# One fused attention and MoE kernel: whole-bank score units, maxima ahead of exponentials, a planner that takes turns at PSUM banks, ten native items

## Chip, cores and metric

The kernel runs on one core of one Trainium2 chip. The metric is device time in microseconds (us): the median over the runs of one kernel. TensorE is called PE here, VectorE DVE, ScalarE ACT, GpSimd POOL and SyncE SP, as in the profile.

## What is computed

Causal-by-block attention for 4 batches of 8 heads (576 positions, head size 64, blocks of 64), then two feed-forward layers over the 2304 tokens: one that takes the largest of three products, one with h * cos(h).

```python
scores = scale * np.matmul(q, k.transpose(0, 1, 3, 2))
mask = (pos[:, None] // 64) >= (pos[None, :] // 64)
scores = np.where(mask, scores, -1e9)
attn = np.exp(scores - scores.max(-1, keepdims=True))
attn = attn / (attn.sum(-1, keepdims=True) + 1e-09)
x = attn @ v                                   # to (2304, 512)
h = np.maximum(np.maximum(x @ w1, x @ w2), x @ w3)   # 512 to 768
x = h @ w_out                                  # 768 to 512
h = x @ w_in                                   # 512 to 2048
out = (h * np.cos(h)) @ w_out2                 # 2048 to 512
```

All inputs are float32, the weights pass as pairs of 32-bit words.

## The kernel before

**Items.** Attention is cut into 32 items: 4 batches, two halves of the query blocks, 4 pairs of heads. `load` fetches q, k and v of an item, two items ahead. `prep` makes operands for the scores. An item with a number under `NATIVE` (line 555) is native: q and k stay float32, k is scaled in place, and a score product is one float32 matmul, which the trace shows as two instructions. Any other item is split: q and k are each divided into a high and a low part in fp32r (`qh`, `ql`, `kh`, `kl`), and a score product is three matmuls, high x high, high x low, low x high. Native q and k (`qnat`, `knat`, two buffers each) lie in the pool `cv_start`. Items 8 to 11, the second batch's first half, have four blocks and 64 to 256 score columns each, 640 in all. Native or not, weights of the MoE layers are also taken apart into high and low parts (`convert`: tiles `raw`, `t`, `whi`, `wlo`), on DVE and ACT, beside attention.

**Scores.** `scores` goes through the tiles of an item. A tile is one or two banks of PSUM (slots `SA`, two banks, and `SB`, one bank), and holds the scores of one to three query blocks. For each block, PE's matmuls are recorded first (in one unit for each block and bank: instructions that the planner keeps together). Then, block by block, DVE takes the maximum (`top`) and ACT the exponential with its row sum (`prob`). Then the rows are scaled by their sums, transposed on PE (`tb`, copied to `pt`), multiplied with v (`X`) and written to `xhi`, `xlo` or, by way of `xs`, to memory.

**Filler.** The first MoE layer's matmuls for 512 tokens (`psm`, two banks) can start once attention has given those tokens; the first 512 are complete after item 7. From then on they fill PE between the parts of attention. Their evictions go to `hm`, in pool `wk`. `wk` is opened when `cv_start` is closed, and a pool closes only after all users of its tiles.

**The planner.** Nothing runs in the order in which it is recorded. `Plan` records operations with their reads and writes, gives each a cost (`price`), and lists them forward and backward in eight passes (`forward`, `backward`); the shortest plan is emitted, each engine's instructions in the planned order. Before the change, two operations depend on each other when the ranges of a tile that they touch overlap and one of them writes. Two reads never do, and a matmul into other columns of a bank doesn't depend on a read of that bank. The semaphores of the program itself are put in by the framework behind the planner, after the emitted order. `COLD` is the time before which the planner counts PE as slow.

Of the kernel before, what the change touches and what calls it, by code (L numbers as in the profile page):

```python
# [19 lines left out]
P = 128  # L20
# [109 lines left out]
class Plan:  # L130
    CROSS = 150.0
    EARLY = 130000.0
    SWITCH = 350.0
    COLD = 7600.0
    SLOW, CROWD, LANDING = 9000.0, 50000.0, 1000.0
    WEIGHT = {"DVE": 2.5, "ACT": 1.0, "POOL": 100.0}

# [38 lines left out]
    def record(self, engine, real, method, args, kw):  # L176
        if self.unit_op == "new" or self.unit_op is None:
            o = self.op(engine)
            if self.unit_op == "new":
                self.unit_op = o  # L180
        else:
            o = self.unit_op
        out = [kw["out"] if "out" in kw else args[0]] + ([kw["accum_out"]] if "accum_out" in kw else [])
        given = [v for v in list(args) + list(kw.values()) if isinstance(v, View)]
        outs = [v for v in out if isinstance(v, View)]
        ins = [v for v in given if not any(v is w for w in outs)]
        for v, write in [(v, False) for v in ins] + [(v, True) for v in outs]:
            b = v.buf
            o.deps |= {x for x, lo, hi in (b.writes + b.reads if write else b.writes)
                       if x is not o and lo <= v.hi and v.lo <= hi}  # L190
            if write:
                if v.hi - v.lo == v.n - 1 and v.rows == b.shape[0] and self.unit_op is None:
                    b.reads = [x for x in b.reads if x[1] < v.lo or x[2] > v.hi]
                    b.writes = [x for x in b.writes if x[1] < v.lo or x[2] > v.hi]
                b.writes.append((o, v.lo, v.hi))
            else:
                b.reads.append((o, v.lo, v.hi))
            if not b.ops or b.ops[-1] is not o:
                b.ops.append(o)
        cost, late, port = self.price(engine, method, outs, ins, kw)  # L200
        o.cost += cost
        o.port = o.port or port
        o.late = max(o.late, late)
        o.bufs |= {v.buf for v in given}
        o.calls.append(self.caller(real, method, args, kw))
        return o
# [39 lines left out]
    def price(self, engine, method, outs, ins, kw):  # L246


        if engine == "SP":
            tiles = outs + ins  # L250
            return 600.0, 2000.0 + sum(v.n * v.rows * 4 for v in tiles[:1]) / 340.0, False
        n = outs[0].n
        if engine == "PE":
            late = 190.0
            if method == "transpose":
                return 109.0, late, False
            dt = ins[0].buf.dt
            if dt == F32:
                return (4 * n / 2.4 + 13) / (2 if outs[0].rows == 64 else 1), late, False
            load = ins[0].n / 1.2  # L260
            return (max(n / 2.4 + 3, 65.0) if dt == BF16 else max(n / 2.4 + 13.5, load)), late, False
        psum = any(v.buf.psum for v in outs + ins)
        if method == "tensor_reduce":
            n = ins[0].n
        spread = 120.0 * (outs[0].hi - outs[0].lo + 1 > n)
        ptr = isinstance(kw.get('scale'), View) or len([v for v in ins if v.n == 1]) > 0
        if engine == "ACT":
            scaled = isinstance(kw.get("scale"), View)
            return (n * 0.833 + spread + (55 if psum else 100) + 95 * ("bias" in kw) + 95 * scaled
                    + 93 * ("accum_out" in kw)), 112.0, False  # L270
        if engine == "DVE":
            sb = [v for v in ins if not v.buf.psum]
            fast = method in ("tensor_copy", "tensor_scalar", "memset") and not psum
            two = method in ("tensor_tensor", "scalar_tensor_tensor") and len(sb) > 1
            if method == "reciprocal":
                return 70.0 + 5 * n, 100.0, False
            if method == 'memset':
                return n * 0.82, 88.0, True
            return n * (0.52 if fast else 1.04) + 68 + spread + (65.0 if fast and len([v for v in ins if v.n == 1]) else 0), 88.0, fast or two
        return (n * 3.3 + 75 if method == "tensor_tensor" else max(400.0, n * 1.04 + 195)), 45.0, method != "memset"  # L280


    ENGINES = ("PE", "DVE", "ACT", "POOL", "SP")
# [17 lines left out]
    def forward(self, rank):  # L301
# [6 lines left out]
        end, chosen, bus, port = {}, {}, 0.0, 0.0  # L308

        def finish(o, start, stop):  # L310
            end[o] = (start, stop)
            for u in self.users[o]:
                missing[u] -= 1
                if not missing[u]:
                    release(u)

        def release(o):
# [14 lines left out]
            load[o.engine] += o.cost  # L332
            heapq.heappush(waiting[o.engine], (at, rank[o], o.order, o))

        for o in self.ops:
            if not o.deps:
                release(o)
        while len(end) < len(self.ops):
            best = None
            for e in free:  # L340
                while waiting[e] and waiting[e][0][0] <= free[e]:
                    at, r, order, o = heapq.heappop(waiting[e])
                    heapq.heappush(ready[e], (r, order, at, o))
                if ready[e]:
                    t, pick = free[e], ready[e][0]
                    if pick[3].port and port > t:
                        others = [x for x in ready[e] if not x[3].port]
                        if others:
                            pick = min(others)
                        else:  # L350
                            t = port
                elif waiting[e]:
                    pick = waiting[e][0]
                    t = max(pick[0], port if pick[3].port else 0.0)
                else:
                    continue
                if best is None or t < best[0]:
                    best = (t, e, pick)
            assert best, "the plan has a cycle"
            t, e, pick = best  # L360
            o = pick[3]
            if ready[e]:
                ready[e].remove(pick)
                heapq.heapify(ready[e])
            else:
                heapq.heappop(waiting[e])
            free[e] = t + self.spent(o, t)
            load[e] -= o.cost
            stop = free[e] + o.late
            if o.port:  # L370
                port = free[e]
            if e == "SP":
                bus = max(bus, t + o.cost)
                bus += (o.late - 2000.0) * (1.22 if bus < self.SLOW else 1.0)
                stop = bus + 2000.0
            finish(o, t, stop)
# [76 lines left out]
def fused_kernel(tc, qk, v2, w1, w2, w3, wout, w_in2, w_out2, out):  # L453
    B, HP, _, S = qk.shape
# [10 lines left out]
    R = Plan(tc)  # L465
# [16 lines left out]
    NROT = 3  # L482
    top = [[const.tile([P, 1], F32, f"top{i}_{j}") for j in range(5)] for i in range(NROT)]
# [6 lines left out]
    parts = [(0, 512)]  # L490
# [51 lines left out]
    for first, last, *tiles in (  # L542
# [5 lines left out]
        f = Half()  # L548
# [3 lines left out]
        f.nj = (last + 1) // 2  # L552
        f.order = [(j, b) for j in range(f.nj) for b in f.blocks if 64 * (b + 1) > 128 * j]
        HALF.append(f)
    NATIVE = 8

    items = []
    for b in range(B):
        for half in range(2):
            for pair in range(HP):  # L560
                it = Item()
# [41 lines left out]
    def scores(it):  # L603
# [4 lines left out]
        for banks, parts in f.tiles:  # L608
            if banks == 2:
                s = ps_x.tile([P, 2, 512], F32, "SA", tag="SA", bufs=1)  # L610
            else:
                s = ps_x.tile([P, 1, 512], F32, "SB" if parts[0][0] % 2 == 0 or it.half else "SA", tag="SB" if banks == 1 else "SA", bufs=1)
            started = {}
            for b, c0, n, c in parts:
                i = b - f.first
                qs = slice(i * P, i * P + P)
                for bank in range(c):
                    ks = slice(bank * n, bank * n + n)
                    prods = [(it.q[:, qs], it.k[:, ks])] if it.native else [
                        (it.qh[:, qs], it.kh[:, ks]), (it.qh[:, qs], it.kl[:, ks]), (it.ql[:, qs], it.kh[:, ks])]  # L620
                    with R.unit():
                        for x, (q, k) in enumerate(prods):
                            R.tensor.matmul(s[:, bank, c0:c0 + n], q, k, start=bank not in started and x == 0,
                                            stop=x == len(prods) - 1, skip_group_check=True)
                        if started.setdefault(bank, R.unit_op) is not R.unit_op:
                            R.unit_op.deps.add(started[bank])
            for b, c0, n, c in parts:
                i = b - f.first
                part = s[:, :, c0:c0 + n] if c == 2 else s[:, 0, c0:c0 + n]
                bias = top[it.n % NROT][i]  # L630
                R.vector.tensor_reduce(bias, part, axis=AX.XY if c == 2 else AX.X, op=ALU.max, negate=True)
                p = prob[b][:, 0:n * c]
                if c == 2:
                    p = p.rearrange("p (c n) -> p c n", c=2)
# [279 lines left out]
    banks = {}  # L914
# [90 lines left out]
```

## Time and profile before

| | us |
|---|---|
| median of 3 runs | 893.03 (892.97 to 894.29) |
| the profiled execution | 893.89 |
| its span, first to last instruction | 892.1 |
| PE busy | 874.9 (98%) |
| DVE busy | 551.4 (62%) |
| ACT busy | 436.3 (49%) |

A busy share is a mean over the whole span: attention and the first MoE layer fill the first 390 us or so, the second MoE layer the rest. PE's busy time counts matmuls from start to modelled end, so an idle gap in it is real, and a busy stretch can still hold lost turns. The waits name who released an engine; a wait of PEld is that of a weight load, which stands in PE's queue in front of its matmul.

### The profile page before, as it was taken

The numbers are of one execution on the slowest core, as the hardware profiler recorded it, in microseconds if no ns is written. First come the engines' busy times: TensorE is split into PE (matmuls) and PEld (weight loads), VectorE is DVE, ScalarE is ACT, GpSimd is POOL, SyncE is SP. The second block draws the span as 40 slices with busy tenths as digits, with TensorE's granted clock in tenths as the row PEclk, the third lists the DMA queues.
The fourth block names the chain that finished last, engine by engine and source line by source line (L and its number), as shares of the span: only waits on it lengthen the run. The fifth ranks groups of instructions, "written<-read, shape, count | busy, mean of one in ns | idle before, by whom it ended". The sixth has DMA issues, their size and how long they took to land.

```text
span 892.1 us, 12461 instructions
## 1 busy us (share of the span) xinstructions
PE 874.9 (98%) x4626; PEld 722.9 (81%) x4626; DVE 551.4 (62%) x1092; ACT 436.3 (49%) x955; POOL 1.2 (0%) x12
## 2 busy tenths in 40 slices
PE   7899999999999999999999999999999999999998
PEld 5567877888878787878889888888888888888897
DVE  5999988874566725629332697655465455455454
ACT  6987687863677717756221543332233223322333
POOL 0000000000000000000000000000000000000000
PEclk9999999999999999999999999999999999999999
DMA  7655645661245702545040751110001000100000
GB/s 238 207 170 171 194 133 189 225 225 71 84 136 189 246 25 59 152 158 173 27 142 6 291 198 50 48 48 1 0 25 48 1 0 1 48 1 0 24 25 24
DMA packets 42396, 90.33 MB, mean 101 GB/s; under 512 B 5728, under 2 KB 15456, under 8 KB 42336
## 3 DMA queue, kind: packets, MB, share of 16 engines
q1 hardware_dynamic: 42336, 89.54, 30.3%
q8 instruction: 36, 0.59, 0.3%
q14 instruction: 24, 0.20, 0.1%
HBM read 69.07 MB, written 20.45 MB: 100 GB/s over the span
## 4 chain that ended last, share of the span: by engine, by line
PE 88%; DVE 6%; ACT 3%; issue 1%; DMA 1%; POOLq 0%; SPq 0%; POOL 0%; ACTq 0%; DVEq 0%
PE psm L211 53%; PE po L211 22%; PE X L211 4%; PE SA L211 4%; PE tb L211 3%; PE SB L211 3%; DVE top L211 2%; ACT prob L211 2%; DVE t L211 2%; DMA q<-qk 1%; DVE prob L211 0%; ACT pt L211 0%; DVE wlo L211 0%; DVE whi L211 0%; DVE ql L211 0%
## 5 line engine op out<-in xcount | busy, mean ns | idle before, releaser
L211 PE MATMUL psm<-yh,w_in 128*128 128x512 f32 (+1 forms) x640 | 194.0, 368 | 0.0
L211 PE MATMUL po<-w_out,gh 128*128 128x512 f32 x576 | 177.8, 390 | 0.0
L211 ACT ACTIVATE th<-th,halfpi 128x512 f32<-128x512 f32 (+1 forms) x80 | 54.6, 683 | 188.8 <-DVE th L211 188.8
L211 PE MATMUL psm<-xhi,whi 128*128 128x512 f32 (+1 forms) x360 | 135.3, 376 | 1.2 <-ACT hm L211 0.7
L211 PEld LDWEIGHTS psm<-yh,w_in 128*128 128x128 f32 x640 | 117.1, 188 | 20.5
L211 PE MATMUL psm<-xlo,whi 128*128 128x512 f32 (+1 forms) x360 | 132.7, 369 | 0.0
L211 PE MATMUL psm<-xhi,wlo 128*128 128x512 f32 (+1 forms) x360 | 132.7, 369 | 0.0
L211 PEld LDWEIGHTS po<-w_out,gh 128*128 128x128 f32 x576 | 107.1, 188 | 21.4
L211 PE MATMUL psm<-yl,w_in 128*128 128x512 f32 (+1 forms) x320 | 117.7, 368 | 0.0
L211 PE MATMUL po<-w_out,gl 128*128 128x512 f32 x288 | 112.0, 389 | 0.0
L211 DVE TENSOR_SCALAR th<-psm 128x512 int32<-128x512 f32 (+1 forms) x80 | 51.0, 638 | 76.1 <-PE psm L211 75.9
L211 DVE TENSOR_TENSOR th<-psm,th 128x512 f32<-128x512 f32 (+1 forms) x80 | 51.0, 638 | 53.8 <-ACT th L211 53.8
L211 DVE TENSOR_TENSOR hm<-psm,hm 128x512 f32<-128x512 f32 (+1 forms) x60 | 38.2, 636 | 68.4 <-PE psm L211 67.9
L211 PEld LDWEIGHTS psm<-xhi,whi 128*128 128x128 f32 x360 | 68.0, 189 | 11.8 <-ACT hm L211 1.2
L211 PEld LDWEIGHTS psm<-xhi,wlo 128*128 128x128 f32 x360 | 67.9, 189 | 11.6
L211 PEld LDWEIGHTS psm<-xlo,whi 128*128 128x128 f32 x360 | 68.0, 189 | 9.8 <-DVE xlo L211 0.2
L211 DVE TENSOR_TENSOR gl<-th,gh 128x512 fp32r<-128x512 f32 (+1 forms) x80 | 50.9, 636 | 38.4 <-ACT gh L211 38.4
L211 ACT CAST gh<-th 128x512 fp32r<-128x512 f32 (+1 forms) x76 | 44.1, 580 | 55.7 <-DVE th L211 55.7
L211 PEld LDWEIGHTS psm<-yl,w_in 128*128 128x128 f32 x320 | 60.3, 189 | 10.6
L211 PEld LDWEIGHTS po<-w_out,gl 128*128 128x128 f32 x288 | 54.1, 188 | 11.3
L211 PE MATMUL tb<-ident,prob 128*128 128x128 f32 x400 | 59.7, 278 | 1.2 <-ACT pt L211 0.6
L211 ACT COPY pt<-tb 128x512 f32<-128x512 f32 (+1 forms) x94 | 51.9, 568 | 16.4 <-PE tb L211 15.9
(96 smaller groups left out, 1322.4 us busy)
## 6 DMA issues: line engine op xcount, KB each, us to landing
raw<-w SPq DMA_DIRECT2D x18, 512.0 KB, 3.5
raw<-w_in SPq DMA_DIRECT2D x16, 512.0 KB, 3.7
raw<-w_out SPq DMA_DIRECT2D x16, 512.0 KB, 4.3
vr<-v SPq DMA_DIRECT2D x16, 320.0 KB, 3.5
kept_in<-both SPq DMA_DIRECT2D x10, 512.0 KB, 3.7
w_in<-kept_in SPq DMA_DIRECT2D x10, 512.0 KB, 9.1
out<-osb SPq DMA_DIRECT2D x18, 256.0 KB, 2.0
y<-hm SPq DMA_DIRECT2D x16, 256.0 KB, 2.5
```

What stands on the lines that cost most here:

```text
L211: return lambda: getattr(real, method)(*[value(a) for a in args], **{k: value(a) for k, a in kw.items()})
```

## The change

Five edits. (1) In `scores` all matmuls of a bank become one unit, whatever blocks they belong to; only the first of them carries the start flag. (2) The maxima of all blocks of a tile are recorded ahead of all exponentials. (3) In `record`, an access to a PSUM tile counts as one to the whole tile, and a read depends on earlier reads by other engines, so the plan lets engines take turns at it. (4) `NATIVE` goes from 8 to 10: items 8 and 9 are native too. (5) Figures of the planner: `COLD` 7600 to 7400, another price for POOL's memset and affine_select; and a counter in place of a length, with no effect on the plan.

```diff
-    COLD = 7600.0
+    COLD = 7400.0
...
             b = v.buf
-            o.deps |= {x for x, lo, hi in (b.writes + b.reads if write else b.writes)
-                       if x is not o and lo <= v.hi and v.lo <= hi}
+            lo, hi = (0, len(b.index)) if b.psum else (v.lo, v.hi)
+            o.deps |= {x for x, x0, x1 in (b.writes + b.reads if write else b.writes)
+                       if x is not o and lo <= x1 and x0 <= hi}
+            if b.psum:
+                o.deps |= {x for x, _, _ in b.reads if x.engine != engine}
...
-        return (n * 3.3 + 75 if method == "tensor_tensor" else max(400.0, n * 1.04 + 195)), 45.0, method != "memset"
+        if method in ("memset", "affine_select"):
+            return n * 1.2 + 90.0, 45.0, False
+        return (n * 3.3 + 75 if method == "tensor_tensor" else max(400.0, n * 1.04 + 195)), 45.0, True
...
-    NATIVE = 8
+    NATIVE = 10
...
-            started = {}
-            for b, c0, n, c in parts:
-                i = b - f.first
-                qs = slice(i * P, i * P + P)
-                for bank in range(c):
-                    ks = slice(bank * n, bank * n + n)
-                    prods = [(it.q[:, qs], it.k[:, ks])] if it.native else [
-                        (it.qh[:, qs], it.kh[:, ks]), (it.qh[:, qs], it.kl[:, ks]), (it.ql[:, qs], it.kh[:, ks])]
-                    with R.unit():
+            for bank in range(s.dims[0][1] if banks == 2 else 1):
+                with R.unit():
+                    first = True
+                    for b, c0, n, c in parts:
+                        ks = slice(bank * n, bank * n + n)
+                        i = b - f.first
+                        qs = slice(i * P, i * P + P)
+                        prods = [(it.q[:, qs], it.k[:, ks])] if it.native else [
+                            (it.qh[:, qs], it.kh[:, ks]), (it.qh[:, qs], it.kl[:, ks]), (it.ql[:, qs], it.kh[:, ks])]
                         for x, (q, k) in enumerate(prods):
-                            R.tensor.matmul(s[:, bank, c0:c0 + n], q, k, start=bank not in started and x == 0,
-                                            stop=x == len(prods) - 1, skip_group_check=True)
-                        if started.setdefault(bank, R.unit_op) is not R.unit_op:
-                            R.unit_op.deps.add(started[bank])
+                            R.tensor.matmul(s[:, bank, c0:c0 + n], q, k, start=first, stop=x == len(prods) - 1,
+                                            skip_group_check=True)
+                            first = False
             for b, c0, n, c in parts:
                 i = b - f.first
                 part = s[:, :, c0:c0 + n] if c == 2 else s[:, 0, c0:c0 + n]
                 bias = top[it.n % NROT][i]
                 R.vector.tensor_reduce(bias, part, axis=AX.XY if c == 2 else AX.X, op=ALU.max, negate=True)
+            for b, c0, n, c in parts:
+                i = b - f.first
+                part = s[:, :, c0:c0 + n] if c == 2 else s[:, 0, c0:c0 + n]
+                bias = top[it.n % NROT][i]
                 p = prob[b][:, 0:n * c]
```

## Rows read from the trace of the kernel before

**Rows 1.** The page, busy time: engine, us, share of the span, instructions.
```profile
PE 874.9 (98%) x4626; PEld 722.9 (81%) x4626; DVE 551.4 (62%) x1092; ACT 436.3 (49%) x955; POOL 1.2 (0%) x12
```

**Rows 2.** Three windows: length, busy time and instructions of each engine, PE clock, DMA.
```profile
0.00:75.00 75.00, 64.62 (x384) 46.73 (x384) 63.80 (x170) 62.86 (x169) 1.17 (x12) 0.98 0.62 205
75.00:400.00 325.00, 321.79 (x1864) 262.36 (x1865) 216.10 (x462) 211.64 (x515) 0.00 (x0) 1.00 0.46 149
400.00:892.00 492.00, 488.46 (x2380) 413.82 (x2378) 271.50 (x462) 161.83 (x274) 0.00 (x0) 1.00 0.16 54
```

**Rows 3.** Chain of waits, first 80 us: shares by engine and tile.
```profile
by line: ACT prob L211 16.1%; DVE t L211 12.7%; DVE top L211 10.7%; PE psm L211 10.0%; PE SA L211 6.9%; issue 5.7%; PE SB L211 5.2%; DVE wlo L211 4.4%; DVE prob L211 4.3%; PE X L211 3.8%; PE tb L211 3.6%; DVE whi L211 2.9%; ACT pt L211 2.3%
```

**Rows 4.** Waits of DVE and of ACT, 0 to 75 us: total, times, longest.
```profile
DVE top L211 <- PE SB L211: 6.7, 1, 6.7
DVE top L211 <- ACT prob L211: 1.9, 3, 0.7
...
ACT prob L211 <- DVE top L211: 4.5, 9, 1.1
```

**Rows 5.** Waits of PE's weight loads at score banks, 75 to 400 us.
```profile
PEld SA L211 <- DVE top L211: 4.2, 8, 0.8
...
PEld SB L211 <- ACT prob L211: 1.1, 3, 0.7
```

**Rows 6.** Timeline, DVE and ACT: start, duration, engine, operation, shapes, count, idle before.
```profile
4.10 0.47 ACT L211 ACTIVATE knat<-knat 128x320 f32<-128x320 f32 x1 [1.87 <-DMA knat<-qk]
...
65.85 0.63 ACT L211 ACTIVATE qh<-q 128x512 fp32r<-128x512 f32 x1
66.85 0.28 DVE L211 CAST kh<-k 128x256 fp32r<-128x256 f32 x1
67.32 0.68 DVE L211 SCALAR_TENSOR_TENSOR ql<-q,qh 128x512 fp32r<-128x512 f32 x1
67.92 0.42 DVE L211 TENSOR_TENSOR kl<-k,kh 128x256 fp32r<-128x256 f32 x1
```

**Rows 7.** Timeline, the first item's score banks.
```profile
7.26 0.53 ACT L211 ACTIVATE prob<-SB,top 128x320 f32<-128x320 f32 x1 [0.48 <-DVE top L211]
7.91 0.36 DVE L211 TENSOR_REDUCE top<-SB 128x1 f32<-128x192 f32 x1 [0.69 <-ACT prob L211]
8.66 0.43 PE L211 MATMUL SA<-knat,qnat 128*128 128x64 f32 x2 [0.97 <-DVE top L211]
11.12 1.97 PE L211 MATMUL SA<-knat,qnat 128*128 128x256 f32 x6 [1.11 <-ACT prob L211]
```

**Rows 8.** Two windows around the stretch at another clock (columns as in rows 2).
```profile
7.30:10.70 3.40, 1.74 (x9) 1.09 (x7) 1.63 (x6) 2.05 (x9) 0.00 (x0) 1.00 0.92 337
10.70:14.10 3.40, 2.98 (x12) 2.81 (x13) 2.58 (x11) 2.29 (x7) 0.00 (x0) 0.50 0.38 127
```

**Rows 9.** Timeline of PE, native score blocks of 256, 128 and 64 columns, what follows.
```profile
18.13 0.99 PE L211 MATMUL SA<-knat,qnat 128*128 128x256 f32 x6
18.95 1.13 PE L211 MATMUL tb<-ident,prob 128*128 128x128 f32 x8
```

**Rows 10.** Timeline, from the last native scores to the first full filler.
```profile
60.83 0.91 PE L211 MATMUL SB<-knat,qnat 128*128 128x384 f32 x2 [0.22 <-ACT prob L211]
69.25 0.28 PE L211 MATMUL SA<-kh,qh 128*128 128x256 f32 x1
...
70.01 1.96 PE L211 MATMUL X<-pt,vr 128*64 128x256 f32 x20
...
72.47 0.28 PE L211 MATMUL SA<-kh,ql 128*128 128x64 f32 x1
...
74.66 0.69 DVE L211 COPY hm<-psm 128x512 f32<-128x512 f32 x1
...
75.40 0.50 PE L211 MATMUL psm<-xhi,whi 128*128 128x512 f32 x1 [0.43 <-DVE hm L211]
```

**Rows 11.** Loads of knat: time from issue to landing.
```profile
DMA to landing us min/median/max: 2.3/3.1/4.3
```

More of the change, by code (lines that the diff above doesn't have):

```diff
@@ L188, in record @@
             b = v.buf
-            o.deps |= {x for x, lo, hi in (b.writes + b.reads if write else b.writes)
-                       if x is not o and lo <= v.hi and v.lo <= hi}
+            lo, hi = (0, len(b.index)) if b.psum else (v.lo, v.hi)
[3 more added lines that the diff above has]
+                o.deps |= {x for x, _, _ in b.reads if x.engine != engine}
             if write:
[L192 to L195, printed above, removed]
+                if hi - lo == v.n - 1 and v.rows == b.shape[0] and self.unit_op is None:
+                    b.reads = [x for x in b.reads if x[1] < lo or x[2] > hi]
+                    b.writes = [x for x in b.writes if x[1] < lo or x[2] > hi]
+                b.writes.append((o, lo, hi))
             else:
-                b.reads.append((o, v.lo, v.hi))
+                b.reads.append((o, lo, hi))
             if not b.ops or b.ops[-1] is not o:
@@ L310, in finish @@
         def finish(o, start, stop):
+            nonlocal left
+            left -= 1
             end[o] = (start, stop)
@@ L333, in release @@
             heapq.heappush(waiting[o.engine], (at, rank[o], o.order, o))
+        left = len(self.ops)
         for o in self.ops:
@@ L337, in forward @@
                 release(o)
-        while len(end) < len(self.ops):
+        while left:
             best = None
```

## The prediction

> **What bounds the kernel now.** The busy table comes first: TensorE (PE) is busy for 874.9 us of a span of 892.1 us [rows 1], so some 17 us are to be had by removing idle time, unless PE gets less to do. The windows say where they lie. From 0 to 75 us PE is busy for 64.62 us, so 10.4 us are idle; from 75 to 400 us 3.2 us are idle; from 400 us on 3.5 us are idle, and the change touches nothing there [rows 2]. The first stretch is the one to read. VectorE (DVE) and ScalarE (ACT) are busy there for 63.80 and 62.86 us of 75 us [rows 2], and DVE's first work, a maximum, waits for 6.7 us [rows 4], so once attention runs both are nearly full. The chain of waits through the first 80 us agrees: ACT's exponentials are 16.1% of it, DVE's weight conversion t 12.7%, DVE's maxima 10.7%, PE's score banks 6.9 and 5.2% [rows 3]. At 75.40 us PE's filler of the first MoE layer starts after its last wait of this stretch [rows 10], and PE stays full. So two things are worth something: reaching that point sooner, which is a matter of DVE, ACT and the hand-overs between them, and losing fewer turns between 75 and 400 us, where filler is ready for any gap.
>
> **Items 8 and 9 native.** Removed for each item: the split of q and k. On DVE that is ql at 0.68 us, kl at 0.42 us, and kh at 0.28 us for one of the two (the other's kh ran on ACT) [rows 6]: 2 x (0.68 + 0.42) + 0.28 = 2.48 us. On ACT it is qh, twice at about 0.63 us [rows 6], plus one kh. Added: a scaling of k in place on ACT, at most 0.47 us each (320 columns there, 256 here) [rows 6]. So ACT is relieved by at least 1.26 - 0.94 = 0.3 us. DVE is the fuller engine, so up to 2.5 us of the first 75 can go. Not all do: conversions in DVE's queue that are not yet due may have given way already. The lower bound is 0 (the removed work lay beside other work), or -0.5 if the two scalings land in front of ACT's exponentials, at 0.47 us. I take 1.5 us, nearer to the upper end, since DVE is 85% busy over the stretch counting its empty first 6.7 us, and 93% after them.
>
> On PE the native form changes little. Blocks of 256, 128 and 64 columns, 448 in all, took six instructions from 18.13 to 18.95 us, 0.82 us [rows 9]; item 9's split blocks of 256 and 192 columns, 448 too, took six from 69.25 to 70.01 us, 0.76 us [rows 10]. An item here has 640 columns, so native costs about 0.06 x 640/448 = 0.1 us more, 0.2 us for two, in a stretch where PE has room; I take 0. The Trainium skill, FP8 and Floating Point Precision, section TensorE Precision Notes, says that true fp32 takes four passes through the array. By that rule alone four passes stand against three products: 640 columns at 2.4 GHz would cost 0.27 us more for each item, 0.53 us for two, an estimate from that page. The rows show less, since the split form's small products cost more than their columns.
>
> **Loads that move.** The split items' q and k had a buffer of their own; native ones wait for that of the item two earlier. Item 9's load can issue only once item 7's last native scores, which start at 60.83 us and take 0.91 us, are done, about 61.8 us [rows 10]; such a load lands in 3.1 us, at most 4.3 [rows 11]; the scaling adds 0.47 us: 65.4 to 66.6 us, while item 9's scores began at 69.25 us [rows 10]. They have 2.7 us in hand. Behind the waiting issue on SP stand weight loads and x stores, which would start as much later; the planner can order them ahead. I take 0.
>
> **Maxima first, one unit for each bank.** In the kernel before, DVE and ACT alternate at a bank: at 7.91 us DVE's second maximum waits 0.69 us for ACT to leave the bank, though it reads other columns, and at 8.66 us PE waits 0.97 us for a DVE read of other columns of its bank [rows 7]. So the program takes turns already; it is the planner that did not know. The new order has one hand-over from DVE to ACT for a bank instead of three or five. Directly visible from 0 to 75 us are 1.9 us in which DVE waits for ACT's exponentials [rows 4]; they would go. ACT's 4.5 us behind the maxima [rows 4] partly stay: its first exponential now waits for the last maximum of the bank, with whatever ACT has queued behind it. I take 0.8 us (bounds -0.4, as the first exponential now waits for one more maximum, 0.36 us for 192 columns [rows 7], to 1.9). For the first item the alternation from 7.26 to 11.12 us [rows 7], when PE gets the bank back, shortens: without PE's 0.97 us for its last 64 columns some of the chain goes. I take 0.5 us (0 to 1.0).
>
> PE's own 10.4 idle us of this stretch [rows 2] are the other side of the same queues, and there is little filler to put in: I count nothing more. From 75 to 400 us filler is there, and PE's loads wait 4.2 us for DVE and 1.1 us for ACT at score banks [rows 5]. A planner that knows the turns puts matmuls of the MoE layer there. Some of those waits overlap the tail of the matmul before, as PE's whole idle time there is 3.2 us [rows 2]; I take 1.2 us (0 to 3.2; below nothing if whole-bank units, now up to 0.76 us long [rows 10], arrive later than the pieces did: -1.0).
>
> **The planner's figures.** The warm-up border, the price of GpSimd's memset and the counter change no instruction, only the order. None of it stands in the chain of the first 80 us beyond the start [rows 3]; I take 0, between -0.5 and +0.5.
>
> **Sum.** 1.5 + 0.8 + 0.5 + 1.2 = 4.0 us. The profiled execution took 893.89 us, 892.1 of span and 1.8 around it: 889.9. It lies 0.86 us above the median of the runs, 893.03, so on the scale of the median the forecast is 889.0 us.
>
> **Rivals.**
> 1. *The stretch at half clock goes as well.* The granted clock is 0.50, which is 1.2 GHz, from 10.70 to 14.10 us, after PE was busy for 1.74 of the 3.40 us before [rows 8]. The six native matmuls at 11.12 us took 1.97 us [rows 7], the same six at 18.13 us 0.99 us [rows 9]: about 1 us, with the transposes behind them some 1.5 us. If shorter turns keep PE busier there, the fall doesn't come, and with PE's turns at the upper end the time is 889.0 - 1.5 - 1.0 = 886.5 us. The Trainium skill, TensorE: Matmul & The Clock Gate, section "HAM oscillation — how this bites in real kernels", has gaps in PE's work bring the half rate back; the rows here show such a fall, once. Against it: PE still waits for the same loads in the first 8 us. Chance 0.16.
> 2. *The relief is swallowed.* DVE stays nearly full with conversions, which the filler needs, and the first MoE group can't finish before item 7 is through, whose chain the change shortens only at its turns. Then only part of the hand-overs and a few PE turns are left, about 0.5 us: 892.5 us. The reordered list loses here and there what it gains. Chance 0.22.
> 3. *Slower: the pool of the native tiles closes later.* It closes after the last native item; the filler's work pool opens in its place, and the first eviction hm needs it. Until now item 7 ended that at about 61.8 us, far ahead of hm at 74.66 us; now item 9 does, whose last matmul started at 72.47 us [rows 10]: 2 us in hand. It decides against the change once item 9's scores end more than 2 us later than in the profile, relative to item 7. PE has two filler banks; behind them it stops. With the items' loads queued behind others and item 9 some 5 us late, PE stands idle for 3 us or more after the hand-over in hand is spent: 893.03 + 3 = 896 us. Chance 0.14. Another 0.04 goes to a second stretch at half clock of some 3.4 us, which would cost up to 1.7 us and give 894.8 or more.
>
> **How the numbers follow.** Forecast 0.44 (own range 887.3 to 891.2), rival 1 0.16, rival 2 0.22, slower 0.18. A measurement of this kernel can tell about 0.2%, 1.8 us, from no change: faster is below 891.2, slower above 894.8. Faster 0.60, same 0.22, slower 0.18. All upper ends together would give 893.0 - 2.5 - 1.9 - 1.0 - 3.2 - 1.5 = 882.9 us, which is unlikely at once; the low end is 884.8. The high end takes in half of the slower case: 895.5.
>
> **What would show it.** In the profile after: no ql, kl, qh or kh for items 8 and 9, and ten scalings of knat; at each bank all maxima before the first exponential, and no DVE wait for ACT in a bank's middle; PE full from about 72 to 73 us instead of 75.4; PE's loads waiting less than 5.3 us at score banks after 75 us; the tail from 400 us on as long as before. I am wrong if PE becomes full no sooner (rival 2), if hm waits for the pool (rival 3), or if PE's idle time between 75 and 400 us grows.

## The result and the profile after

The changed kernel takes 885.67 us (median of 5 runs, 885.22 to 886.62) against 893.18 us before (892.97 to 894.29): a ratio of 0.9915, 95% interval 0.9901 to 0.9928, or 7.5 us less. The forecast was 889.0 us, 4.0 us less. The profiled execution took 885.22 us, with a span of 883.4 us, 8.7 us shorter than before.

Where the time came from is first read from windows of the changed kernel, to be held against [rows 2] (columns as there).

```profile
0.00:75.00 75.00, 63.32 (x391) 46.79 (x392) 66.89 (x178) 67.23 (x181) 1.17 (x12) 1.00 0.71 226
75.00:400.00 325.00, 325.00 (x1889) 267.76 (x1888) 209.11 (x445) 216.81 (x524) 0.00 (x0) 1.00 0.47 147
```

From 75 to 400 us PE has no idle time left, 3.2 us less than before. The first 75 us look no better: PE is busy for 63.32 us there, before for 64.62. But part of the old busy time was matmuls at half clock [rows 7, 8]; here the clock is 1.00 in both windows. The waits of PE's weight loads from 75 to 400 us (total, times, longest) answer to [rows 5]:

```profile
PEld X L214 <- issue: 6.4, 18, 0.4
PEld psm L214 <- issue: 0.3, 2, 0.2
PEld tb L214 <- issue: 0.3, 2, 0.2
PEld psm L214 <- ACT prob L214: 0.2, 1, 0.2
PEld SA L214 <- issue: 0.2, 1, 0.2
```

Nothing waits for a score bank's reader any more; before it was 5.3 us. The start of the changed kernel's timeline answers to [rows 7]:

```profile
6.08 0.75 DVE L214 TENSOR_REDUCE top<-SB 128x1 f32<-128x320 f32 x2 [6.08 <-PE SB L214]
6.87 0.53 ACT L214 ACTIVATE prob<-SB,top 128x320 f32<-128x320 f32 x1 [1.13 <-DVE top L214]
6.91 0.75 DVE L214 TENSOR_REDUCE top<-SA 128x1 f32<-128x256 f32 x3
...
9.04 0.95 PEld L214 LDWEIGHTS SA<-knat,qnat 128*128 128x128 f32 x6 [0.27 <-ACT prob L214]
```

All maxima of a bank come before its first exponential, and PE has the bank back at 9.04 us; before that was at 11.12 us. Of these 2.1 us, 0.65 us were gained before the first maximum, which starts at 6.08 us and before at 6.73 us.

PE's busy time hides lost turns, since a matmul counts until its modelled end, which lies some 0.16 us behind the point at which the next one could start (0.39 us for 512 columns, with the next start after 0.227 us). So a second measure is used below, worked out from all of PE's rows: the time from one matmul's start to the next one's, less what its kind takes in an undisturbed row of the same (0.227 us for 512 columns, 0.12 us for 256, 0.109 us for a transpose, 0.216 us for a native pass of 256 columns), summed over a stretch. Call it PE's lost time. What matmuls take longer at half clock counts in it. With other rows taken as undisturbed a whole column of the table below shifts, by 1 to 4 us, and differences between kernels by 0.5 us at most. Before it is 20.8 us in the first 80 us and 14.2 us from 80 to 400 us; after 18.7 and 7.9 us. So 2.1 us came from the first stretch and 6.3 us from the second; the rest of the kernel loses 0.4 us in both, and from the last attention matmul to the end both take 500.6 us (391.5 to 892.1, and 382.8 to 883.4).

**What the lost 6.3 us were.** The kernel before shows it at one two-bank tile (timeline):

```profile
114.65 0.29 PE L211 MATMUL SA<-kh,ql 128*128 128x288 f32 x1
...
115.00 0.27 PE L211 MATMUL SA<-kh,ql 128*128 128x224 f32 x1
...
115.53 0.75 DVE L211 TENSOR_REDUCE top<-SA 128x1 f32<-128x576 f32 x1
...
116.33 0.19 PEld L211 LDWEIGHTS SA<-kh,qh 128*128 128x128 f32 x1 [0.80 <-DVE top L211]
116.33 0.37 PE L211 MATMUL SA<-kh,qh 128*128 128x224 f32 x1 [0.36 <-DVE top L211]
...
116.97 0.74 ACT L211 ACTIVATE prob<-SA,top 128x576 f32<-128x576 f32 x1 [0.51 <-PE SA L211]
...
117.83 0.63 DVE L211 TENSOR_REDUCE top<-SA 128x1 f32<-128x448 f32 x1 [0.96 <-ACT prob L211]
```

The plan put the last three of the tile's matmuls (one bank's part of the second block, 224 columns) behind three filler matmuls, since it held them free to overlap with the first block's maximum, which reads other columns. The program doesn't let them: PE's weight load waits 0.80 us for DVE's read to end, the exponential then waits 0.51 us for PE, and the second maximum 0.96 us for the exponential. PE itself seems idle for 0.36 us only. Its lost time there lies between the two: from 115.58 to 116.33 us, less 0.227 us, is 0.52 us. In the changed kernel the twelve matmuls of such a tile stand together, from 110.86 to 112.32 us, and none of them waits:

```profile
110.86 0.29 PE L214 MATMUL SA<-kh,qh 128*128 128x288 f32 x1
...
112.20 0.27 PE L214 MATMUL SA<-kh,ql 128*128 128x224 f32 x1
...
112.64 1.28 DVE L214 TENSOR_REDUCE top<-SA 128x1 f32<-128x576 f32 x2
```

Not all of the 6.3 us is of this kind. By the same measure some 5.1 us of it lie ahead of score matmuls. Another 0.9 us lie ahead of fillers, most of it one wait for an eviction hm at 291.1 us that stands in the list of weight load waits of before, 75 to 400 us, and not in that of the changed kernel:

```profile
PEld psm L211 <- ACT hm L211: 1.2, 1, 1.2
```

### The profile page after: what moved, and what is told of

It is laid out like the page before. It is cut to its first block, busy times and chain, and to the rows that moved or that the text cites. A ratio compares the mean times of both kernels' runs of the same rounds, so it can differ in the third digit from the quotient of the medians.

```text
span 883.4 us, 12430 instructions
## 1 busy us (share of the span) xinstructions
PE 868.1 (98%) x4618; PEld 721.1 (82%) x4618; DVE 540.9 (61%) x1072; ACT 440.7 (50%) x969; POOL 1.2 (0%) x12
## 4 chain that ended last, share of the span: by engine, by line
PE 93%; DVE 3%; ACT 2%; DMA 1%; issue 0%; POOLq 0%; POOL 0%; ACTq 0%
PE psm L214 56%; PE po L214 22%; PE X L214 4%; PE tb L214 4%; PE SA L214 4%; PE SB L214 3%; ACT prob L214 1%; DVE t L214 1%; DVE top L214 1%; DMA raw<-w 0%; ACT pt L214 0%; DVE prob L214 0%; DMA knat<-qk 0%; ACT t L214 0%; DVE whi L214 0%
## 5 line engine op out<-in xcount | busy, mean ns | idle before, releaser
L214 PEld LDWEIGHTS psm<-yh,w_in 128*128 128x128 f32 x640 | 117.1, 188 | 20.8
L214 PE MATMUL tb<-ident,prob 128*128 128x128 f32 x400 | 57.6, 276 | 2.6 <-ACT pt L214 1.8
```

The lines of the kernel that those rows point to most:

```text
L214: return lambda: getattr(real, method)(*[value(a) for a in args], **{k: value(a) for k, a in kw.items()})
```

## The experiments

Twelve kernels ran, each timed beside the kernel before on its own chip. Ratios are to that kernel, whose medians were 893.18 to 894.09 us; since chips differ a little, kernels are compared by their ratios, 0.001 being 0.9 us. Lost time and clock are those of the profiled execution.

| kernel | median us | ratio, 95% interval | lost 0-80 us | lost 80-400 us | clock, 0-80 us |
|---|---|---|---|---|---|
| before | 893.18 | 1 | 20.8 | 14.2 | 0.98 |
| changed | 885.67 | 0.9915 (0.9901 to 0.9928) | 18.7 | 7.9 | 1.00 |
| changed, planner without turns | 883.56 | 0.9882 (0.9866 to 0.9897) | 16.8 | 8.1 | 1.00 |
| changed, eight native | 887.70 | 0.9931 (0.9913 to 0.9950) | 20.1 | 8.0 | 0.98 |
| changed, alternating | 892.44 | 0.9978 (0.9967 to 0.9989) | 26.5 | 8.4 | 0.94 |
| changed, block units | 885.12 | 0.9900 (0.9883 to 0.9918) | 19.8 | 8.4 | 0.96 |
| changed, COLD 7600 | 887.74 | 0.9944 (0.9933 to 0.9956) | 23.1 | 8.0 | 0.94 |
| changed, twelve native | 886.40 | 0.9920 (0.9907 to 0.9933) | 20.6 | 7.5 | 0.98 |
| before + maxima first | 893.64 | 0.9996 (0.9982 to 1.0010) | 20.3 | 13.4 | 1.00 |
| before + turns | 893.66 | 0.9993 (0.9979 to 1.0007) | 26.0 | 8.7 | 0.94 |
| before + ten native | 892.61 | 0.9988 (0.9974 to 1.0003) | 22.3 | 13.2 | 0.96 |
| before + figures | 889.10 | 0.9946 (0.9927 to 0.9965) | 19.9 | 12.4 | 0.98 |
| before + units | 886.88 | 0.9927 (0.9915 to 0.9939) | 19.2 | 8.8 | 1.00 |
| before + units and maxima | 886.86 | 0.9939 (0.9920 to 0.9957) | 22.6 | 9.4 | 0.96 |

A profiled execution is not always its kernel's median: those with COLD 7600, with figures, and with units and maxima took 889.78, 891.27 and 891.07 us, about 2 to 4 us above their medians. Their first column is read with that in mind.

The clock has a price of its own, and executions of one kernel show it. Of the kernel before on one chip, the eleven with a mean clock of 1.000 over the span took 892.15 to 893.19 us, the three with 0.994 took 896.92 to 897.77 us. With turns alone, the one with 0.998 took 891.94 us, the three with 0.992 took 894.97 to 895.63 us. That is some 0.6 us for each 0.001 of the mean clock, an estimate from these executions, and about 3.5 us for the 10.2 us at half clock that the profiles of three kernels show in the first 80 us (alternating, COLD 7600, and turns alone: 0.94 in the table).

**First theory: the planner's knowledge of turns.** The first reading of the traces was that PE's lost time after 80 us fell because the planner now knows that engines take turns. Its rivals were the forecast's own (DVE and ACT relieved early) and chance (any new order is some us away from any other). Four kernels each undo one part.

In `record`, the changed lines replaced by the old ones:

```diff
-            lo, hi = (0, len(b.index)) if b.psum else (v.lo, v.hi)
...
-            if b.psum:
-                o.deps |= {x for x, _, _ in b.reads if x.engine != engine}
```

> The changed kernel with its record of PSUM accesses put back to that of the kernel before: the planner again lets a matmul, a maximum and an exponential overlap at a bank. Units, order of maxima and ten native items stay. Turn theory (most of the gain is PE's lost starts between 80 and 400 us, which the planner fills once it knows the turns): 5 to 6 us of the 7.5 go, 890.5 to 892 us, and PE's idle time from 75 to 400 us is 2 us or more again. Relief theory (DVE and ACT relieved in the first 75 us, as forecast): 1 to 2 us go, 887 to 888 us. List-luck theory (any new plan lands within some 3 us of any other): anywhere from 884 to 892 us, without PE's idle time coming back.

It is faster than the changed kernel, 883.56 us, by 2.9 us on the ratios, with intervals that don't meet. The lost time after 80 us stays at 8.1 us. The first theory falls: turns in the plan are not what saved it.

```diff
-    NATIVE = 10
+    NATIVE = 8
```

> The changed kernel with eight native items instead of ten. Relief theory: 1.5 to 2.5 us go, 887.2 to 888.2 us, and PE becomes full that much later. Turn theory: the split of items 8 and 9 lies beside other work, at most 0.8 us go, 885.3 to 886.5 us; PE's idle time from 75 to 400 us stays near 0.

1.4 us slower on the ratios, but the intervals overlap, and its profiled execution had a stretch at half clock, which the changed kernel's had not. The size is just under the relief theory's lower end; by itself this doesn't settle it.

The second loop over the blocks taken out, so that each exponential follows its own maximum:

```diff
-            for b, c0, n, c in parts:
-                i = b - f.first
-                part = s[:, :, c0:c0 + n] if c == 2 else s[:, 0, c0:c0 + n]
-                bias = top[it.n % NROT][i]
                 p = prob[b][:, 0:n * c]
```

> The changed kernel with each exponential recorded right behind its own maximum again, so that DVE and ACT alternate at a bank; the planner still knows the turns. Hand-over theory (fewer hand-overs shorten the bank's hold): 0.8 to 2 us go, 886.5 to 887.7 us, with DVE waits for ACT's exponentials back at 2 us or more before 75 us. Turn theory: the planner knows the longer hold and fills it, within 0.5 us of the changed kernel after 80 us; only the first 75 us grow, by at most 1 us.

A gain of 2.0 us is left of 7.6, by the ratios. No theory had that. After 80 us it loses 8.4 us, as the changed kernel does; the whole difference lies before, 26.5 against 18.7 us. But not in more waiting of DVE: DVE's waits for exponentials in the first 80 us are 1.1 us, less than before. The windows show both engines with less done (the first 80 us of this kernel):

```profile
0.00:80.00 80.00, 66.14 (x372) 47.12 (x373) 68.12 (x172) 69.11 (x181) 1.17 (x12) 0.94 0.66 211
```

And the changed kernel:

```profile
0.00:80.00 80.00, 68.32 (x413) 50.91 (x414) 71.89 (x189) 71.46 (x190) 1.17 (x12) 1.00 0.69 219
```

DVE does 17 instructions fewer, ACT 9, PE 41, at a lower clock. The clock is only part of it: the one execution of this kernel with a mean clock of 1.000 took 890.42 us, against 885.22 to 885.83 us of the changed kernel at that clock.

The old unit for each block and bank, with its `started` table, put back:

```diff
-            for bank in range(s.dims[0][1] if banks == 2 else 1):
-                with R.unit():
...
+            started = {}
+            for b, c0, n, c in parts:
...
+                for bank in range(c):
...
+                    with R.unit():
```

> The changed kernel with one unit for each block and bank, as before, instead of one for a whole bank. Turn theory: the blocks of a bank wait for the same readers either way, so the pieces are put next to each other: within 0.5 us, 885.2 to 886.2 us. If whole-bank units themselves save PE's lost starts, 1 to 3 us go, 886.7 to 888.7 us. If they arrive later than pieces would, it is up to 1 us faster, 884.7 us.

885.12 us, just under the turn theory's range, with an interval that overlaps the changed kernel's: with turns in the plan, units are not needed either. So either of two edits removes the loss after 80 us, and undoing just one of them can't show what it is worth. They had to be tried alone.

**Second theory: split banks.** Four kernels add one edit to the kernel before.

Maxima first alone (the second loop of the change):

> The kernel before with one edit alone: all maxima of a tile recorded ahead of its exponentials. Hand-over theory (the alternation of DVE and ACT at a bank, which the planner of before does not know, is what costs): most of the gain is there, 886 to 888.5 us, and PE's idle time from 75 to 400 us falls from 3.2 us to under 0.5. Turn theory (the planner's knowledge is needed): 891 us or more. Luck theory (any new plan differs by some us): anywhere from 885 to 896, with 1 us or more of idle time left after 75 us.

Nothing: 893.64 us. The weight loads still wait at score banks from 75 to 400 us:

```profile
PEld X L211 <- issue: 5.3, 16, 0.4
PEld SA L211 <- DVE top L211: 4.1, 8, 0.8
...
PEld SB L211 <- ACT prob L211: 1.1, 3, 0.7
```

That is [rows 5] again, within 0.1 us. Fewer hand-overs at a bank don't help while its matmuls are still split.

Turns alone (the change's lines in `record`):

> The kernel before with one edit alone: PSUM accesses count for the whole tile and engines take turns in the plan. Hand-over theory: the planner now sees the alternation, so PE's idle time from 75 to 400 us goes (under 0.5 us), but the first 75 us keep the alternation and get no shorter: 888 to 892 us. Turn theory as first held: 886 to 888 us. Luck theory: anywhere from 885 to 896.

893.66 us. The loss after 80 us does go, from 14.2 to 8.7 us, and the waits at score banks with it:

```profile
PEld X L214 <- issue: 5.8, 17, 0.4
PEld psm L214 <- ACT hm L214: 0.8, 1, 0.8
PEld SA L214 <- ACT prob L214: 0.5, 3, 0.2
```

But the first 80 us lose 26.0 us instead of 20.8, as in the alternating kernel. Both have turns in the plan and exponentials that alternate with maxima. In both the first eviction hm comes late, at 80.7 and 80.9 us, where before it came at 74.66 us [rows 10]. The chain of waits through this kernel's first 80 us, to be held against [rows 3]:

```profile
by line: DVE t L214 25.5%; DVE top L214 14.4%; DVE wlo L214 8.9%; DMA raw<-w 8.2%; DVE prob L214 6.7%; issue 5.4%; DVE xlo L214 3.6%; SPq L214 3.2%; PE tb L214 3.0%; DVE whi L214 2.9%; PE X L214 2.7%; DVE pt L214 2.0%; DVE sums L214 1.8%; P
```

DVE's weight conversions (t) have doubled their share of the chain, and ACT's exponentials, 16.1% before, are not among the shares shown, down to 1.8%: a reading is that the plan put attention behind conversions in the stretch where nothing else can fill PE. The alternating kernel doesn't bear that out: by the same view DVE's t has 13.1% there and ACT's exponentials 8.6%. The clock has a share as well. Eleven of the twelve executions with turns alone had a mean clock of 0.992 to 0.996, where the median of before on that chip was 0.998; the one with 0.998 took 891.94 us, and those of before with 0.998 took 893.02 to 894.87 us. So at a like clock turns alone may be worth 1 to 3 us, which one execution can't settle.

Ten native items alone (`NATIVE = 10`):

> The kernel before with ten native items as its one edit. Relief theory: 1.5 to 2.5 us faster, 890.5 to 892 us on the scale of 893.2 to 894.1 for before, all of it in the first 75 us; PE's idle time from 75 to 400 us stays near 3.2 us. Luck theory: 888 to 898 us, with the idle time after 75 us changed by over 1 us.

892.61 us, 0.12% faster, which the interval doesn't tell from nothing. In the profiled execution the stretch at half clock is longer than before, and the first 80 us lose 22.3 us. At a mean clock of 1.000 its three executions took 891.88 to 892.27 us, those of before on that chip 892.15 to 893.19 us.

The figures alone (`COLD = 7400.0`, the new price of memset and affine_select), meant as a control:

> The kernel before with only the planner's figures changed (the warm-up border and the price of GpSimd's memset): a control, since nothing that runs is changed but the order. If such a change of order is worth nothing, within 0.5 us of before, and PE's idle time from 75 to 400 us is 2.7 to 3.7 us. Luck theory: 2 to 4 us away from before on either side.

The control is 4.8 us faster. Nothing in it runs differently but the order. About 1 us of that can be the clock: at a mean clock of 1.000 its executions took 888.86 to 889.10 us, those of before on that chip 892.15 to 893.19 us. So a new order by itself is worth several us here, and differences of 2 to 4 us between the kernels of this table can't be put down to what an edit does, unless a row shows it. This holds for the native items too.

**What is left, tried alone.** The last four.

Whole-bank units alone:

> The kernel before with one edit alone: all matmuls of a bank in one unit. Split-bank theory (what PE lost after 80 us is a bank whose matmuls the plan splits, with the second part behind a maximum of the first): PE's starts lose some 8 us from 80 to 400 us instead of 14, its weight loads no longer wait 5.3 us at score banks, and with the first 80 us as before the kernel takes 886.5 to 889 us. If the units need the maxima ahead of the exponentials to help, it stays at 891 us or more, with waits of 3 us or more left.

886.88 us, inside the split-bank theory's range: nearly all of the gain from one edit. Lost time after 80 us 8.8 us, and the waits at score banks are down to 0.6 us:

```profile
PEld X L211 <- issue: 5.3, 15, 0.4
PEld SB L211 <- ACT prob L211: 0.6, 2, 0.4
```

The table sorts by it. The four kernels whose plan may split a bank's matmuls (before, and with maxima, native items or figures alone) lose 12.4 to 14.2 us from 80 to 400 us; the ten that have units, or turns, or both lose 7.5 to 9.4 us.

Units and maxima first, without the rest:

> The kernel before with two edits: whole-bank units and maxima first; the planner doesn't know the turns, eight native items, old figures. Split-bank theory: as with the units alone after 80 us (a loss of some 8 us), and the first 80 us 0 to 3 us shorter through the hand-overs: 884 to 888 us. If it is as fast as the changed kernel (885.7) or faster, the planner's knowledge of turns is worth nothing once these two are in. If turns are needed too: 889 us or more.

886.86 us, the same as with units alone. Maxima first adds nothing that can be measured to units. It is worth much only where the plan knows the turns: there it takes the ratio from 0.9978 to 0.9915, 5.6 us, of which the clock can be 1 us or so (890.42 us at a mean clock of 1.000, as said above).

The changed kernel with `COLD = 7600.0`:

> The changed kernel with the planner's warm-up border back at 7600: a control, only the order of the first stretch can differ. If the first 80 us of a plan are a matter of luck by some us, 883.5 to 889 us with the difference before 80 us and the loss after 80 us at 8 us as in the changed kernel; if not, within 0.5 us of 885.7.

2.6 us slower, all of it before 80 us (23.1 against 18.7 us lost, 8.0 against 7.9 after), and the intervals don't meet. But its five executions all had a mean clock of 0.994 to 0.996, those of the changed kernel 0.998 to 1.000, and its profile has this stretch (columns as in [rows 2]):

```profile
11.55:21.79 10.24, 8.70 (x32) 6.31 (x32) 8.96 (x30) 7.82 (x23) 0.00 (x0) 0.50 0.68 203
```

By the price above, 0.004 of the mean clock is some 2.5 us, so the half clock can be all of the difference. What this control shows is that a figure which changes no work can bring a longer stretch at half clock.

The changed kernel with `NATIVE = 12`, the forecast's slower case:

> The changed kernel with twelve native items: the forecast's slower case, made on purpose. The pool of native tiles now closes only after item 11's scores, so the first eviction hm must wait for them. If that is a real price, hm starts some 8 us later than in the changed kernel (72.80 us) and PE, whose filler has two banks, stands idle meanwhile: 887 to 892 us. If the planner brings items 10 and 11 forward or fills PE with their work, within 1 us of 885.7.

886.40 us, 0.4 us more on the ratios, with overlapping intervals. The hand-over is there. The last seven matmuls of the native items, from 76.80 us on, now end just ahead of the first eviction, which comes at 78.22 us instead of 72.80 us:

```profile
76.80 1.09 PE L214 MATMUL SA<-knat,qnat 128*128 128x256 f32 x7
...
78.22 0.62 ACT L214 COPY hm<-psm 128x512 f32<-128x512 f32 x1
```

But PE doesn't stand idle for those 5 us: scores, transposes and products of items 10 and 11 fill them, and its lost time before 80 us grows by 1.9 us, part of that at half clock.

**The fastest version** is the changed kernel without turns in its plan: 883.56 us, 0.9882 of before, against 0.9915 for the change. It has units, maxima first, ten native items and the new figures.

## Why the prediction was right, and where it was not

**Direction and range.** Faster was forecast with 0.60; 885.67 us lies inside 884.8 to 895.5 us. The size was nearly twice the forecast's, and the case that it is nearest to is rival 1, 886.5 us, which had 0.16: the stretch at half clock went, and PE's turns came beyond the upper end. That the number lies so near is in part luck. The half clock isn't what made the size: 20 of 58 executions of the kernel before, on three chips, had a mean clock of 1.000 too, and took 892.15 to 893.29 us, still some 7 us more than the changed kernel's 885.22 to 885.83 us at that clock. And the rival's sum takes 1.0 us for the step from 1.2 us to the upper end of 3.2 us, which is 2.0 us; done rightly it gives 885.5 us.

**PE's turns between 75 and 400 us: the mis-sized term.** It stood in the sum with 1.2 us, bounded by 3.2; it measured 6.3 us of lost time. The step that failed is the cap. A row with about the right size was there, 5.3 us of weight loads waiting at score banks [rows 5], near the 5.1 us that PE lost ahead of score matmuls, and it was cut down because PE's idle time in that stretch was only 3.2 us [rows 2]. Idle time is no bound: PE's busy time runs on through the tail of the last matmul, 0.16 us for 512 columns, which hides that part of a wait. The tile at 116.33 us shows both numbers of one wait, 0.80 us at the load and 0.36 us at the matmul, with 0.52 us lost: the load's wait is no exact measure either. The Trainium skill, Trainium Kernel Development and Optimization, section Performance Expectations, says that matmul busy time is a bad metric of how close a kernel is to its roofline, because matmuls are pipelined. The trace agrees: PE was 98% busy before and after.

The mechanism was named half right. The text had the planner fill the waits with filler because it knows the turns. Turns alone do that, but so do units alone, without any knowledge of turns, and the units were priced only as a possible loss of 1.0 us.

**The first stretch.** Its three terms had 2.8 us of the forecast's 4.0. The profiled executions show 2.1 us less lost time before 80 us, and some 1.2 us of that is the half clock of before (3.4 us of it, at the price above), which stood in a rival and not in the sum. So what the sum named there came out at about 1 us, an estimate: these terms were too large while PE's turns were too small, and part of the one error covered the other.

**Maxima first.** 0.8 us and 0.5 us were taken from fewer hand-overs. The rows changed as said: DVE's waits for exponentials before 75 us are gone (1.9 us [rows 4]), and PE has the first item's bank back 2.1 us sooner. The time did not: alone, and on top of units, it is worth nothing that can be measured. The first item's gain did not last: by item 7's product with v the changed kernel is 1.7 us ahead (68.31 against 70.01 us [rows 10]), with the half clock gone as well. That the edit is worth 5.6 us beside turns in the plan was not foreseen at all.

**Ten native items.** 1.5 us were taken. Undoing it costs 1.4 us and adding it alone gains 1.1 us, neither clear of zero. The forecast's size is neither shown nor ruled out, since an order changed by figures alone moves as much.

**The planner's figures** were given between -0.5 and +0.5 us. That was wrong: 4.8 us alone in the kernel before, and 2.6 us for the border alone in the changed one, the latter with more half clock.

**Slower by the pool of native tiles.** With ten items it didn't come: the first hm is at 72.80 us, sooner than before. With twelve it came as described, five us later, and cost 0.4 us on the ratios, not 3: PE had other work.

**Half clock.** The rival gave about 1.5 us for it. Four of the changed kernel's runs had a mean clock of 1.000 and took 885.22 to 885.83 us; one had 0.998 and took 886.62 us, about 1 us more. So the rival's price is borne out, but the stretch comes and goes with the execution in the kernel before too.

**What stays open.** Why one order of the first 80 us is better than another, from 16.8 us of lost time to 26.5, is shown only in part. The half clock is one part: by the price above it is some 3.5 us in the three kernels with 0.94 in the table, 1.2 us in the kernel before and nothing in the fastest, so about 6 of the 9.7 us between the extremes are left (an estimate). The two kernels with turns and alternating exponentials stay the worst by that reckoning, at some 23 us. What made the planner choose so there, why some orders bring more half clock, and why a cheaper memset with a border of 7400 finds a better order in the kernel before, was not settled. DVE's conversions ahead of attention and later loads each appear in some of the slower kernels, and no run took one of them away alone.

## What to carry to other kernels

Where a planner or a scheduler orders instructions by ranges of a tile, but the program guards a PSUM bank as a whole, make all matmuls of a bank one unit: a part left behind a reader costs PE, the exponential and the next maximum a wait each. Price such waits by the time from one matmul's start to the next, or by the waits of PE's weight loads, not by PE's idle time. And before a few us are put down to an edit of a kernel whose order is planned, change a figure that changes nothing but the order, see how far that moves the time, and compare executions at the same mean clock.

## What the runs showed of the hardware

The clock of PE in the first 80 us differs between kernels and between executions of one kernel: mean 0.94 to 1.00 in the table, at the level of 1.2 GHz wherever it fell. The stretches can be longer than that of the kernel before; from 11.70 to 21.90 us the kernel with turns alone ran at half clock (columns as in [rows 2]):

```profile
11.70:21.90 10.20, 8.11 (x31) 5.31 (x30) 8.88 (x25) 9.41 (x27) 0.00 (x0) 0.50 0.63 207
```

PE got through 31 matmuls there, 3.0 per us; from 21.90 to 80 us, at clock 1.00, it got through 322, 5.5 per us; other kinds of matmul and waits are in both numbers. The fastest kernel's profiled execution has no such stretch. Reads at one bank are kept apart by the program even between two readers: [rows 7] has DVE's read of 192 columns wait 0.69 us for ACT's read of 320 others. The Trainium skill, PSUM — Partial Sum Buffer, section "PSUM bank collisions raise a hardware error", states a reason for that, that any two engines at one bank and quadrant at once collide, two reads included. The trace shows only that they take turns, and no run here let them meet.
